# adaLN decode block with cached GQA attention: w_mod loaded over two DMA queues by halves of the partitions, and the last two parts of wo loaded as one transfer

## The chip, the cores and the metric

The kernel runs on one core of one Trainium2 chip. The metric is the device time of one execution in microseconds. The engines are named as in the profile: PE (TensorE), DVE (VectorE), ACT (ScalarE), POOL (GpSimd) and SP (SyncE). SP does no arithmetic here; it issues DMAs.

## What is computed

One token goes through a transformer block in decode. A modulation vector comes from a condition `c`; attention has 32 query heads over 8 KV heads with a cache of 32768 positions; a ReLU feed-forward part follows. All inputs are bf16. The k and v caches are 64 MB each and make up nearly all of the bytes.

```python
x = A_x                                              # [1, 1, 512]
mod = (silu(c) @ w_mod).reshape(1, 6, 1, 512)        # w_mod [512, 3072]
sa, ca, ga, sb, cb, gb = (mod[:, i] for i in range(6))
h = layernorm(x) * (1 + ca) + sa
q = (h @ wq) -> 32 heads of 128                      # wq [512, 4096]
scores = q @ k.T * 128 ** -0.5                       # k, v [8, 32768, 128], 4 query heads share one
o = softmax(scores) @ v
x = x + ga * (o @ wo)                                # wo [4096, 512]
h = layernorm(x) * (1 + cb) + sb
x = x + gb * (relu(h @ w1) @ w2)                     # w1 [512, 1792], w2 [1792, 512]
```

## The kernel before

**The stream.** All large tensors come in one fixed order, the list `stream` (L139 to L144): `w_mod`, `wq`, the two halves of head 0's K, then for each head in turn half of the next head's K and half of this head's V, at the end the last V in three pieces, `wo` in four parts (`WOP`, L47: heads 0 to 3, 4 and 5, 6, 7), `w1` in two and `w2` in six. `need(key)` (L147) issues loads in this order until the wanted one has been issued. Each load is one DMA from SP (`stream_dma`, L131, the DMA at L132) into one of five slots of 32 KB per partition (`ring`, L74). A slot's next load waits on SP until the last user of the slot is done. A K or V half is 4096 KB: 128 partitions of 32 KB each, contiguous in memory. `w_mod` is 3072 KB: partition p holds rows 4p to 4p + 3, 24,576 contiguous bytes. A wo part of one head is 512 KB: 4096 bytes for each partition. Completion of SP's and ACT's DMAs is counted on eight semaphores taken in turn, so a DMA may also wait for the one eight places before it.

**The head.** While `w_mod` comes, POOL loads `c` and `x` as small rows (L156, L157), DVE builds masks, and PE turns c and x into columns (L227). ACT and DVE make `siluT` (L284 to L289), PE multiplies it with `w_mod` (`to_rows`, L295), and rows become columns again (L313). The first layer norm gives `hT` (L278), PE multiplies it with `wq` (L362), and `qrep_sb` (L377) holds q. ACT writes q into a block-diagonal operand `qbd` for each head (`build_qbd`, L389).

**The heads.** For each K half DVE transposes four pieces in place (`turn_k`, L405), PE forms scores (`scores`, L422), DVE takes them out with their maximum (L428), and a softmax with one exponential (L459) and one transpose (L465) gives `PT_g`. P·V is 32 matmuls for each half of V (`pv`, L484), in a loop on PE's sequencer for all but the last pieces. The order on PE and DVE is written out by hand in L599 to L742: scores of head g + 1 run between the parts of head g.

**The tail.** After the last V, `project(i)` multiplies the heads of part i with their part of `wo`. Parts 0 and 1 use it as the moving operand (L561), parts 2 and 3 as the weights that are loaded into PE (L567). `keep_clock(n)` puts n filler matmuls (L597) between these steps. Then come the second norm, `w1` (L714), the ReLU (L725), `w2` (L735) and the output DMA (L743).

Of the kernel before, what the change touches and what calls it, by code (L numbers as in the profile page):

```python
# [17 lines left out]
def kernel(  # L18
# [14 lines left out]
    nc = tc.nc  # L33
    P = 128
    _, _, D = A_x.shape
    _, Hkv, Sk, Dh = A_k_cache.shape
    Hq = A_wq.shape[1] // Dh
    REP = Hq // Hkv
# [8 lines left out]
    WOP = [(0, Hkv // 2), (Hkv // 2, Hkv // 4), (Hkv - 2, 1), (Hkv - 1, 1)]  # L47
    WOROWS = 2
    LAST = Hkv - 1
# [11 lines left out]
    vv = A_v_cache[0].rearrange("g (p j) d -> g p j d", p=P)  # L61
    wm_v = w_mod.rearrange("(p kt) n -> p kt n", p=P)
    wq_v = A_wq.rearrange("(p kt) n -> p kt n", p=P)
    def wo_v(i):
        g0, n = WOP[i]
        return A_wo[g0 * REP * Dh:(g0 + n) * REP * Dh, :].rearrange("(p r) d -> p r d", p=P)

    w1_v = B_w1.rearrange("(p kt) f -> p kt f", p=P)
    w2_v = B_w2.rearrange("(p f) d -> p f d", p=P)

# [15 lines left out]
    loaded, last_loop = {}, []  # L86
# [3 lines left out]
    def piece(name, at, n):  # L90

        if name not in pieces:
            pieces[name] = ring.tile([P, 2 * TK * Dh], BF16, tag="slot", name=name)
        return pieces[name][:, at:at + n]

    def load(key):
        kind = key[0]
        if kind == "wm":
            t = ring.tile([P, KT, 6 * D], BF16, tag="slot", name="wm_sb")
            src = wm_v  # L100
        elif kind == "wq":
            t = ring.tile([P, KT, Hq * Dh], BF16, tag="slot", name="wq_sb")
            src = wq_v
        elif kind in "kv":
            g, steps = key[1], key[2]
            src = (kv if kind == "k" else vv)[g, :, TK * steps[0]:TK * (steps[-1] + 1), :]
            name = "Ksb" if kind == "k" else "Vsb"
            if len(steps) == 2:
                t = ring.tile([P, TK * len(steps), Dh], BF16, tag="slot", name=name)
            else:  # L110
                t = piece(name, TK * Dh * (steps[0] % 2), TK * Dh).rearrange("p (j d) -> p j d", d=Dh)
        elif kind == "wo":
            g0, n = WOP[key[1]]
            t = piece("wo_sb", g0 * REP * D, n * REP * D).rearrange("p (r d) -> p r d", d=D)
            src = wo_v(key[1])
        elif kind == "w1":
            k0, k1 = W1P[key[1]]
            t = piece("w12_sb", k0 * Dff, (k1 - k0) * Dff).rearrange("p (kt f) -> p kt f", f=Dff)
            src = w1_v[:, k0:k1]
        else:  # L120
            f0, f1 = W2P[key[1]]
            t = piece("w12_sb", KT * Dff + f0 * D, (f1 - f0) * D).rearrange("p (f d) -> p f d", d=D)
            src = w2_v[:, f0:f1]
        stream_dma(t[:], src)
        if kind in "kv":
            for i, u in enumerate(steps):
                loaded[(kind, g, u)] = t[:, TK * i:TK * (i + 1), :]
        else:
            loaded[key] = t[:]

    def stream_dma(dst, src):  # L131
        i = nc.sync.dma_start(out=dst, in_=src)  # L132
        tc.stamp_issue_order_token(i.ins, "sp_stream")
        if last_loop:

            tc.add_manual_dep(i.ins, last_loop[0], mybir.DependencyInfo(
                mybir.DependencyClass.NoSync, mybir.DependencyReason.DATA))

    stream = [("wm",), ("wq",)] + [("k", 0, (2 * G, 2 * G + 1)) for G in range(NG)]  # L139
    for g in range(LAST):  # L140
        for G in range(NG):
            stream += [(kind, gg, (2 * G, 2 * G + 1)) for kind, gg in (("k", g + 1), ("v", g))]
    stream += [("v", LAST, (0, 1)), ("v", LAST, (2,)), ("v", LAST, (3,))] + [("wo", i) for i in range(len(WOP))]
    stream += [("w1", i) for i in range(len(W1P))] + [("w2", i) for i in range(len(W2P))]  # L144
    pos = [0]

    def need(key):  # L147
        while key not in loaded:
            load(stream[pos[0]])
            pos[0] += 1  # L150
        return loaded[key]
# [17 lines left out]
    for hp in range(4):  # L169
        h, par = hp // 2, hp % 2  # L170
        src = AP(ib.tensor, ib.offset + 64 * h + par, [[ib.ap[0][0], P], [0, 4], [2, 32]])
# [8 lines left out]
        out=mask4, in_=ident_f[:].rearrange("p (x q) -> p q x", q=REP), op=ALU.add, axis=AX.X,  # L180
# [3 lines left out]
    for n in sorted({n * REP for _, n in WOP}):  # L184
        cmask[n] = const.tile([P, P // n], F32, name=f"cmask{n}")
        nc.vector.tensor_reduce(
            out=cmask[n][:], in_=ident_f[:].rearrange("p (c r) -> p c r", r=n), op=ALU.add, axis=AX.X,
# [3 lines left out]
            out=rsel_f[:], in_=ident_f[:].rearrange("p (c r) -> p r c", r=n), op=ALU.add, axis=AX.X,  # L191
# [6 lines left out]
        out=smask[:], in_=ident_f[0:16, 0:16].rearrange("p (s q) -> p s q", q=REP), op=ALU.add, axis=AX.X,  # L198
# [8 lines left out]
        out=place32[:], in_=ident_f[:].rearrange("p (j m) -> p m j", m=32), op=ALU.add, axis=AX.X,  # L207
# [3 lines left out]
        out=rowpick[:], in_=ident_f[:].rearrange("p (j m) -> p j m", m=32), op=ALU.add, axis=AX.X,  # L211
# [10 lines left out]
        out=cx_bd[:], in0=cx_row[:].unsqueeze(1).to_broadcast([16, 8, D // 8]),  # L222
# [108 lines left out]
    def four_rows(e, name):  # L331
# [15 lines left out]
        out=nca[:], in0=modT_sb[:, KT:2 * KT], scalar1=-1.0, scalar2=-1.0, op0=ALU.mult, op1=ALU.add,  # L347
# [3 lines left out]
        out=ncb[:], in0=modT_sb[:, 4 * KT:5 * KT], scalar1=-1.0, scalar2=-1.0, op0=ALU.mult, op1=ALU.add,  # L351
# [16 lines left out]
    for i in range(2):  # L368
        nc.vector.transpose(out=q_cols[:, i, :], in_=q_ps[i])
        nc.scalar.copy(  # L370
            out=qT_sb[:, 16 * i:16 * (i + 1)], in_=q_cols[:, i, :].rearrange("p (h r) -> p h r", r=32)[:, :, 0],
# [227 lines left out]
    with tc.manual_schedule(engines={mybir.EngineType.PE, mybir.EngineType.DVE}):  # L599
# [11 lines left out]
        for g in range(LAST):  # L611
# [81 lines left out]
            out=x1T[:], in0=x1T[:], scalar=1.0, in1=xT, op0=ALU.mult, op1=ALU.add, accum_out=stat2[:, 0:1],  # L693
# [29 lines left out]
        for f0, f1 in ((0, FT // 2), (FT // 2, FT)):  # L723
            nc.vector.transpose(out=hidT[:, f0:f1], in_=hid_v[:, f0:f1])  # L724
            nc.scalar.activation(  # L725
                out=AP(hb.tensor, hb.offset + KT * KT * f0, [hb.ap[0], [KT * KT, f1 - f0], [KT + 1, KT]]),
                in_=hidT[:, f0:f1, 0:1].to_broadcast([P, f1 - f0, KT]), func=ACT.Relu,
# [46 lines left out]
```

## Time and profile before

| | |
|---|---|
| Runs | 355.38, 355.42, 355.53 us; median 355.42 |
| The profiled execution | 355.74 us, its span 353.9 us |
| Busy | PE 279.8 us (79%), DVE 203.1 (57%), ACT 25.4 (7%), POOL 3.9 (1%) |
| DMA | 149.59 MB, mean 423 GB/s |
| Granted PE clock | 0.947 mean |
| w_mod | one issue from SP, 3072 KB, 10.4 us to landing |
| wq | 4096 KB, 19.6 us to landing |
| wo | 2048, 1024 and twice 512 KB; 29.1, 31.1 and 32.3 us (median of the two) to landing |

The span runs from the first to the last instruction; the time of an execution holds a little more around it. A line of the timeline gives start, duration, engine, line of the kernel, operation, output and inputs, count, and in brackets the idle time before and what ended it. A line of the windows gives the stretch, its length, busy time and number of instructions for PE, PEld (weight loads), DVE, ACT and POOL, then the granted clock, the DMA share and GB/s.

### The profile page before, as it was taken

Reading aid. Unit: us, or ns where it says so; the run is one execution under the profiler, and the core shown is the slowest. Engines: PE = TensorE matmul, PEld = TensorE weight load, DVE = VectorE, ACT = ScalarE, POOL = GpSimd, SP = SyncE. Lnnn points to the kernel's source line nnn. Section 1 sums busy time; section 2 is a strip of 40 time slices with the busy share of each in tenths; the row PEclk is TensorE's granted clock in tenths of the full one; section 3 lists DMA queues with packets and bytes.
Section 4 is the critical chain, followed back from the end, with each engine's and each line's share of the span. In section 5 each row is a group of like instructions: output and inputs, shape, how many; then the busy total and the mean of one; then the engine's idle time right before and its main releaser. Section 6 shows DMA issues by size and latency. Waiting matters only on the chain. (4 is left out here: it accounts for less than half of the span.)

```text
span 353.9 us, 4006 instructions
## 1 busy us (share of the span) xinstructions
PE 279.8 (79%) x1311; PEld 112.7 (32%) x1311; DVE 203.1 (57%) x271; ACT 25.4 (7%) x69; POOL 3.9 (1%) x16
## 2 busy tenths in 40 slices
PE   0542781999898979897979796979689687989996
PEld 0221230333343323332323232323234233334444
DVE  6245775882768268462939178553938095734142
ACT  1220003000010001000100001000100010002000
POOL 4000000000000000000000000000000000000000
PEclk9995997799899999998999899999999997999999
DMA  8999999999999999999999999999999999999994
GB/s 309 455 422 445 431 422 441 441 418 424 459 418 422 459 418 424 441 437 426 433 444 417 430 456 419 427 446 426 422 448 430 422 439 441 422 430 424 421 420 177
DMA packets 6852, 149.59 MB, mean 423 GB/s; under 512 B 824, under 2 KB 1080, under 8 KB 1976
## 3 DMA queue, kind: packets, MB, share of 16 engines
q1 hardware_dynamic: 6776, 149.43, 98.4%
q8 instruction: 8, 0.13, 0.1%
q14 instruction: 4, 0.03, 0.0%
q0 software_dynamic: 64, 0.00, 0.0%
HBM read 149.42 MB, written 0.00 MB: 422 GB/s over the span
## 5 line engine op out<-in xcount | busy, mean ns | idle before, releaser
L405 DVE STREAM_TRANSPOSE Ksb<-Ksb 128x2048 f32<-128x2048 f32 x64 | 142.9, 2281 | 63.9 <-DMA Ksb<-in_A_k_cache_dram 63.9
L484 PE MATMUL o_ps<-Vsb,PT_g 128*16 (+1 forms) x512 | 130.0, 395 | 21.5 <-ACT qbd L389 7.2
L422 PE MATMUL S_ps<-Ksb,qbd 128*128 128x512 bf16 x512 | 121.8, 388 | 23.5 <-DVE Ksb L405 21.9
L422 PEld LDWEIGHTS <-qbd 128*128 128x128 bf16 x512 | 49.0, 98 | 87.6 <-issue 31.8
L484 PEld LDWEIGHTS o_ps<-Vsb,PT_g 128*16 x416 | 37.4, 90 | 90.2 <-issue 63.7
L428 DVE TENSOR_SCALAR_CACHE_REDUCE S_g<-S_ps 128x512 f32<-128x512 f32 x16 | 11.0, 690 | 34.4 <-PE S_ps L422 34.4
L389 ACT COPY qbd<-qrep_sb 32x16 bf16<-32x16 bf16 x32 | 6.4, 201 | 138.7 <-PE S_ps L422 137.6
L465 DVE STREAM_TRANSPOSE PT_g<-P_g 128x1024 bf16<-128x1024 bf16 x8 | 9.7, 1218 | 6.6 <-ACT P_g L459 6.6
L484 PEld LDWEIGHTS <-PT_g 128*16 128x16 bf16 x96 | 8.2, 90 | 11.0
L456 ACT ACTIVATE nbias<-Mb_ps 128x1 f32<-128x1 f32 x8 | 1.4, 171 | 136.8 <-PE Mb_ps L454 136.8
L459 ACT ACTIVATE P_g<-S_g,nbias 128x1024 bf16<-128x1024 f32 x8 | 9.2, 1148 | 0.2
L227 PE MATMUL xc_ps<-cx_sel,cx_bd 16*128 16x2 bf16 x4 | 0.3, 172 | 11.1 <-DVE cx_bd L221 11.1
L515 DVE SCALAR_TENSOR_TENSOR Y<-o_ps,smask,Y 16x128 f32<-16x128 f32 x24 | 8.1, 339 | 0.8
L471 PE MATMUL L_ps<-Lexp,ones_f 128*128 128x4 f32 x16 | 3.0, 257 | 4.3 <-DVE Lexp L468 4.3
L597 PE MATMUL spare_ps<-qbd,ident_bf 128*128 128x512 bf16 x19 | 5.6, 380 | 0.0
L440 PE MATMUL mT_ps<-ident_f,m_p 128*1 128x128 f32 x8 | 2.2, 270 | 3.9 <-DVE m_p L437 2.0
L471 PEld LDWEIGHTS L_ps<-Lexp,ones_f 128*128 128x128 f32 x16 | 3.1, 221 | 5.8 <-issue 5.1
L443 DVE TENSOR_REDUCE Mrow<-mT_ps 1x4 f32<-1x128 f32 x8 | 2.1, 257 | 4.6 <-PE mT_ps L440 4.6
L534 DVE TENSOR_TENSOR oT_sb<-acc_ps,Linv 128x4 bf16<-128x4 f32 x8 | 1.2, 150 | 5.7 <-PE acc_ps L521 5.7
L295 PE MATMUL mod_ps<-wm_sb,siluT 128*1 128x512 bf16 x24 | 3.6, 624 | 1.0 <-DVE siluT L289 1.0
L505 DVE MEMSET o_ps<- 16x512 f32 x8 | 3.9, 485 | 0.8
L552 DVE CAST o_sb<-o_ps 128x4 bf16<-128x4 f32 (+2 forms) x4 | 0.7, 167 | 5.7 <-PE o_ps L548 5.7
(115 smaller groups left out, 80.0 us busy)
## 6 DMA issues: line engine op xcount, KB each, us to landing
Ksb<-in_A_k_cache_dram SPq DMA_DIRECT2D x16, 4096.0 KB, 35.6
Vsb<-in_A_v_cache_dram SPq DMA_DIRECT2D x15, 4096.0 KB, 35.2
wq_sb<-in_A_wq_dram SPq DMA_DIRECT2D x1, 4096.0 KB, 19.6
Vsb<-in_A_v_cache_dram SPq DMA_DIRECT2D x2, 2048.0 KB, 31.8
wm_sb<-in_w_mod_dram SPq DMA_DIRECT2D x1, 3072.0 KB, 10.4
wo_sb<-in_A_wo_dram SPq DMA_DIRECT2D x1, 2048.0 KB, 29.1
w_sb<-in_B_w_dram SPq DMA_DIRECT2D x1, 1344.0 KB
wo_sb<-in_A_wo_dram SPq DMA_DIRECT2D x1, 1024.0 KB, 31.1
```

Of the source, the lines that this page charges most:

```text
L295: nc.tensor.matmul(dst[j // 4][32 * (j % 4):32 * (j % 4) + 1, :], lhsT=src_T[:, kt:kt + 1], rhs=w[:, kt, j * 512:(j + 1) * 512], start=(kt ...
L389: nc.scalar.copy(out=o, in_=i)
L405: t = nc.vector.transpose(out=KTt.bitcast(F32), in_=KTt.bitcast(F32))
L422: nc.tensor.matmul(S_ps_tiles[g], lhsT=qbd[g % 2][:, hp, 4 * (7 - s):4 * (7 - s) + P], rhs=KTv[:, 16 * sl:16 * sl + 16, h, :, par], start= ...
L428: nc.vector.tensor_scalar(out=S_tiles[g][:, G, :], in0=S_ps_tiles[g], scalar1=1.0, scalar2=None, op0=ALU.mult, op1=ALU.max, accum_out=m_ti ...
L459: nc.scalar.activation(out=P_g[:], in_=S_g[:].rearrange("p g f -> p (g f)"), func=ACT.Exp, bias=nbias[:], scale=scale, accum_out=l_g[:],)
L465: nc.vector.transpose(out=PT_g[:], in_=P_g[:])
L471: nc.tensor.matmul(L_ps[:], lhsT=ones_f[:], rhs=Lexp[:], start=True, stop=True)
L484: nc.tensor.matmul(o_tiles[g][:], lhsT=PT, rhs=Vx, start=False, stop=False, skip_group_check=True)
L505: nc.vector.memset(o_tiles[g][:], 0.0)
L515: nc.vector.scalar_tensor_tensor(out=Y[:], in0=o[:, s], scalar=smask[:, s:s + 1], in1=Y[:], op0=ALU.mult, op1=ALU.add,)
L597: nc.tensor.matmul(spare[0], lhsT=ident_bf[:], rhs=qbd[0][:, :, 0:P], start=True, stop=True)
```

## The change

`w_mod` is loaded by two DMAs: SP takes partitions 0 to 63, and ACT, as its first instruction, partitions 64 to 127. Each partition's bytes are the same. The parts 2 and 3 of `wo` (heads 6 and 7, 512 KB each) come as one transfer of 1024 KB, 128 partitions with two runs of 4096 bytes each. The total number of DMAs from SP and ACT stays the same. The instructions of PE, DVE and POOL and their order are unchanged; ACT has the one DMA more. Lines below the edit are four higher in the changed kernel.

```diff
-    def wo_v(i):
-        g0, n = WOP[i]
-        return A_wo[g0 * REP * Dh:(g0 + n) * REP * Dh, :].rearrange("(p r) d -> p r d", p=P)
-
...
         elif kind == "wo":
-            g0, n = WOP[key[1]]
-            t = piece("wo_sb", g0 * REP * D, n * REP * D).rearrange("p (r d) -> p r d", d=D)
-            src = wo_v(key[1])
+            parts = key[1]
+            (g0, n), m = WOP[parts[0]], len(parts)
+            t = piece("wo_sb", g0 * REP * D, m * n * REP * D).rearrange("p (g x) -> p g x", g=m)
+            src = A_wo[g0 * REP * Dh:(g0 + m * n) * REP * Dh, :].rearrange("(g p r) d -> p g (r d)", g=m, p=P)
...
-        stream_dma(t[:], src)
+        if kind == "wm":
+            stream_dma(t[0:P // 2], src[0:P // 2])
+            nc.scalar.dma_start(out=t[P // 2:P], in_=src[P // 2:P])
+        else:
+            stream_dma(t[:], src)
...
+        elif kind == "wo":
+            for m, i in enumerate(parts):
+                loaded[("wo", i)] = t[:, m].rearrange("p (r d) -> p r d", d=D)
...
-    stream += [("v", LAST, (0, 1)), ("v", LAST, (2,)), ("v", LAST, (3,))] + [("wo", i) for i in range(len(WOP))]
+    stream += [("v", LAST, (0, 1)), ("v", LAST, (2,)), ("v", LAST, (3,))] + [("wo", parts) for parts in ((0,), (1,), (2, 3))]
```

## Prediction

> **What bounds the kernel now.** I began with the page's queue summary and its line of DMA shares, then cut the first microseconds and the long middle into windows, and last read the timeline and the waits around the two places that the change touches.
>
> ```profile
> q1 hardware_dynamic: 6776, 149.43, 98.4%
> ...
> 30.00:100.00 70.00, 51.63 (x201) 20.03 (x202) 48.09 (x38) 4.30 (x12) 0.00 (x0) 0.86 1.01 433
> 100.00:200.00 100.00, 86.88 (x371) 34.33 (x369) 62.30 (x70) 6.66 (x21) 0.00 (x0) 0.98 1.00 433
> 200.00:300.00 100.00, 82.49 (x340) 32.17 (x340) 59.49 (x70) 5.04 (x13) 0.00 (x0) 0.96 1.00 432
> ```
>
> One queue, SP's, carries all the bulk data and keeps its 16 DMA engines busy for 98.4% of the span. In the windows the last two columns are the DMA share and GB/s: 433 GB/s from 30 to 300 us, 27.1 GB/s for each engine, with no hole. A 4096 KB transfer lands 35 us after its issue, so three or four are always queued. Whatever delays this stream delays all behind it, one for one.
>
> The timeline shows how the stream becomes the end:
>
> ```profile
> 283.51 6.70 DVE L405 STREAM_TRANSPOSE Ksb<-Ksb 128x2048 f32<-128x2048 f32 x3 [7.53 <-DMA Ksb<-in_A_k_cache_dram]
> ...
> 298.65 4.63 PE L484 MATMUL o_ps<-Vsb,PT_g 128*16 x12 [0.66 <-PE L_ps L471]
> ...
> 302.99 2.31 DVE L405 STREAM_TRANSPOSE Ksb<-Ksb 128x2048 f32<-128x2048 f32 x1 [4.50 <-DMA Ksb<-in_A_k_cache_dram]
> ```
>
> DVE stands idle 7.53 us for head 7's first half of K, and at 283.51 starts on it. From there one chain of DVE and PE work runs to the output DMA at 351.84 us: transposes, the softmax of head 6, its P·V loop from 298.65, scores, the last P·V, the projections and the feed-forward part. So the end is the landing of that K plus some 68 us. The last K half (302.99) is covered: its scores begin only at 307.78.
>
> **The head: w_mod over two queues.** Before, one 3072 KB transfer, issued at 0.74 us and landed 10.4 us later. Now SP issues 64 partitions and ACT the other 64. The number of bytes does not change, and neither does SP's issue count here (one DMA, 0.40 us).
>
> ACT gets one DMA issue in front of its table load. Queued behind it are that load (0.74 to 2.02 us before) and the exponential of L284, which starts at 11.58 after 9.56 us of idle; an issue of 0.4 us costs nothing there. Without that cover it would cost its 0.4 us.
>
> The half transfers also make two landings where SP's first V load and PE's w_mod matmuls waited for one. The V load went out at 17.13 us with w_q and three K halves queued, good until about 40 us; a delay of 10 us is covered. The PE matmuls wait today for siluT at 13.52, 2.4 us after w_mod at 11.1.
>
> The two small rows c and x (GpSimd's queue, landing at 8.4 and 10.2 us) have to share the engines with one more queue. The third queue is there only until w_mod has landed, so their 8.3 us can grow by a few, not double; siluT, hT and q would move with them. In the timeline q is spread into qbd by 26.80, while PE's first scores wait for K, landed and transposed, until 32.79: 6 us of cover, which grows with every delay of the stream. I cost it at nothing; beyond the 6 us each would cost one at the first scores.
>
> That leaves what two half-width transfers do to the stream itself. These windows of a quarter microsecond show its start (a packet is counted where it starts):
>
> ```profile
> 1.75:2.00 0.25, 0.00 (x0) 0.00 (x0) 0.23 (x1) 0.25 (x1) 0.25 (x2) 1.00 5.36 1278
> 2.00:2.25 0.25, 0.00 (x0) 0.00 (x0) 0.00 (x0) 0.02 (x1) 0.25 (x1) 1.00 1.53 295
> ...
> 4.00:4.25 0.25, 0.00 (x0) 0.00 (x0) 0.25 (x2) 0.00 (x0) 0.25 (x2) 1.00 0.23 98
> 4.25:4.50 0.25, 0.00 (x0) 0.00 (x0) 0.25 (x2) 0.00 (x0) 0.25 (x1) 1.00 2.28 983
> 4.50:4.75 0.25, 0.00 (x0) 0.00 (x0) 0.25 (x2) 0.00 (x0) 0.25 (x3) 1.00 1.14 492
> 4.75:5.00 0.25, 0.00 (x0) 0.00 (x0) 0.25 (x2) 0.00 (x0) 0.24 (x2) 1.00 0.00 0
> ```
>
> Read as bytes, the first two rows are 393 KB, and so are the three from 4.00: 16 rows of w_mod (24,576 bytes each), one for each engine. The engines march in step: a wave starts within half a microsecond, then nothing starts until the next. At 27.1 GB/s a row lasts 0.91 us, and w_mod is eight rows for each engine, 7.27 us.
>
> Before, each wave went to partitions of both halves. Now, if all 16 engines take a row from SP's queue, the wave goes to partitions 0 to 63 only, and the next, from ACT's, to 64 to 127 only. No row of the trace shows a large transfer over 64 partitions, so I bound it. From below: if only the engines limit, nothing is lost, and something could be won at the cold start (a rival below). From above: no transfer here ever gave a partition more than its 1/128 of 433 GB/s. If that is a limit of the receiving side, a wave over half of the partitions takes twice as long, 8 x 0.91 = 7.3 us in all. Engines that share a destination collide less the further they are apart: half a microsecond, the width of a wave, would leave 0.41 of 0.91 us of loss in each row, 3.3 us in all. I take the middle of 3.3 and 7.3, 5.3 us, because waves this narrow put both queues' rows in step, and because a transfer has landed only when its slowest engine is done.
>
> The Trainium skill, page "SBUF — State Buffer", section "Door 1: The DMA port swizzle", states that partitions 0 to 63 reach only 8 of 16 SBUF ports (196 GB/s measured for them), and that two concurrent transfers, at partition 0 and partition 64, gave just 6% more than one. By that, an estimate, 3.15 MB at 208 GB/s would take 15.1 us and the head lose 7.9 us; this trace has nothing that could confirm it.
>
> **The tail: wo's two last parts in one transfer.** One issue fewer for SP. The bytes stay, and their place in the queue. SP's later issues move up (they wait for one of eight completion slots, and these now count one transfer further back), but the last of them still waits for this very transfer, and the queue is full anyway: nothing.
>
> What changes is when the second last part is known to have landed. Before, the four wo loads were issued from 307.8 to 309.1 and took 29.1 to 32.7 us, so the last landed at 309.1 + 32.7 = 341.8. The part before it is 512 KB shorter in line, 1.2 us at 433 GB/s: 340.6. Its user:
>
> ```profile
> 341.20 0.59 PE L597 MATMUL spare_ps<-qbd,ident_bf 128*128 128x512 bf16 x2
> ...
> 341.42 0.80 PEld L567 LDWEIGHTS <-wo_sb 128*128 128x128 bf16 x16
> ```
>
> These weight loads begin at 341.42, inside the filler matmuls that end at 341.80. Merged, they cannot begin before 341.8: between 0.1 us (the filler covers most) and 0.45 us (0.38 and a weight load) are added. Queued behind them on PE are project(2), the joining of rows, project(3), the norm and the feed-forward matmuls; nothing absorbs it, and the output waits for all. I take 0.3 us, nearer to the upper end, as the loads had run ahead of the filler by 0.38. The stream and this chain move together, so this holds whatever the head does.
>
> **Sum.** The profiled execution took 355.74 us, 1.8 more than its span and 0.32 above the median. 355.74 + 5.3 + 0.3 = 361.3; against the median 355.42 + 5.6 = **361.0 us**. Own range of this case: 355.42 + 3.3 + 0.1 to 355.42 + 7.3 + 0.45, 358.8 to 363.2.
>
> **Rivals.** *The halves cost the stream nothing* (0.25). For it: an engine's 27.1 GB/s is the same for every size of row, which fits a limit in the engines; then eight rows per engine are eight rows, from whichever queue. The Trainium skill, page "DMA: Bandwidth & Descriptors", section "Issuing engines are not separate DMA queues", says that the same 16 engines serve all issuers and that only issue time is saved; the 98.4% on one queue and the 0.40 us issue agree with that. The time is 355.42 + 0.3 = 355.7 (355.2 to 356.3). Against it: narrow waves, as above.
>
> *The cold start shrinks* (0.12), the other side. The first wave starts at 1.75, and the third only at 4.25, where two rows at 0.91 would have put it at 3.6; and w_mod lands at 11.1, where 1.75 + 7.27 is 9.0. Up to 2.1 us of start are lost on the slowest engine. If a second queue's row is fetched while the first is still cold, part of that comes back. With 1.2 us won and 0.3 lost the time is 354.5; it is faster by over 0.2% from 1.0 us won on. At its end, 2.1, it is 353.6. Against it: the following row of the same queue could be fetched ahead as well, and the gap is there all the same.
>
> *The engines fall out of step early* (0.08): after one or two rows some take SP's half while others take ACT's, and only 0.9 to 2.3 us are lost: 356.6 to 358.0.
>
> One thing widens every case by up to 1 us: the granted clock was 0.50 from 296 to 300 us, on the chain to the end (eight scores took 2.77 us there, 1.90 elsewhere); a moved start can move that dip.
>
> **How the numbers follow.** Collision 0.55, nothing 0.25, cold start 0.12, out of step 0.08. The forecast is the likeliest, 361.0. The range, 355.0 to 363.2, holds the collision, the second case and the one out of step, and leaves out the cold start and edges, under 2 in 10. About 0.2%, 0.7 us, is what a measurement of this kernel can tell from no change. Faster by more: 0.12. Within it: 0.22, nearly all of the second case. Slower: 0.66, the collision, out of step, and 0.03 of the second.
>
> **What would show it.** Right: w_mod's landing near 16 us instead of 11.1, windows from 2 to 16 us well under 400 GB/s, the first transpose of K near 36 instead of 30.48, and the wait for head 7's K ending near 289 instead of 283.51; the span from there to the output up by 0.3, with the wo_sb weight loads after the landing. Wrong: w_mod landed by 11 us at 400 GB/s and over, which leaves only the tail; or K's first transpose before 30 us, which is the cold start. The tail is wrong if the output still comes 68.3 us after that K wait.

## The result: 363.29 us, 2.2% slower

The changed kernel takes 363.29 us (median of six runs, 361.87 to 364.51) against 355.40 for the kernel before (355.23 to 355.53); the ratio is 1.0225 with a 95% interval of 1.0213 to 1.0238. That is 7.9 us. The direction and the place were forecast, the size was not: 361.0 with an upper end of 363.2. The profiled execution took 363.29 us with a span of 361.5, so the two profiled executions differ by 7.55 us.

**The profile after.** The queue summary of the changed kernel has a second row, ACT's queue:

```profile
q1 hardware_dynamic: 6696, 147.85, 96.3%
q10 hardware_dynamic: 80, 1.57, 2.0%
```

One window over the head of the kernel before, and then the windows of the changed kernel (last columns: granted clock, DMA share, GB/s):

```profile
4.75:9.75 5.00, 0.00 (x0) 0.00 (x0) 3.27 (x19) 0.00 (x0) 0.24 (x2) 1.00 0.94 400
```

```profile
4.75:9.75 5.00, 0.00 (x0) 0.00 (x0) 3.27 (x19) 0.00 (x0) 0.24 (x2) 1.00 0.97 211
...
12.00:14.00 2.00, 0.00 (x0) 0.00 (x0) 0.00 (x0) 0.00 (x0) 0.00 (x0) 1.00 0.97 197
14.00:16.00 2.00, 0.00 (x0) 0.00 (x0) 0.00 (x0) 0.00 (x0) 0.00 (x0) 1.00 0.97 197
...
2.75:16.00 13.25, 0.00 (x0) 0.00 (x0) 4.89 (x19) 0.00 (x0) 2.23 (x9) 1.00 1.02 217
```

Here the two columns part company. The DMA share is 0.97, so by that column all engines are busy; but they move 197 to 211 GB/s in these windows and 217 on average, where the kernel before moved 400 in the window 4.75 to 9.75. A busy DMA engine is not one at its rate; GB/s has to be read beside the share. In windows of a quarter microsecond a row of w_mod is seen to take twice its time:

```profile
5.50:5.75 0.25, 0.00 (x0) 0.00 (x0) 0.25 (x2) 0.00 (x0) 0.00 (x0) 1.00 4.34 885
...
6.25:6.50 0.25, 0.00 (x0) 0.00 (x0) 0.25 (x3) 0.00 (x0) 0.00 (x0) 1.00 1.85 393
...
7.25:7.50 0.25, 0.00 (x0) 0.00 (x0) 0.25 (x3) 0.00 (x0) 0.00 (x0) 1.00 2.65 590
7.50:7.75 0.25, 0.00 (x0) 0.00 (x0) 0.25 (x3) 0.00 (x0) 0.00 (x0) 1.00 1.76 393
```

A packet is counted, with its bytes and its time, in the window in which it starts. At 5.50 the 885 GB/s are nine rows of 24,576 bytes, and the share of 4.34 is 4.34 x 0.25 us x 16 engines, 17.4 us in all: 1.93 us a row. The six rows at 7.25 come to 1.77 us each; before, a row took 0.91. So it is not that half of the engines stand idle: all 16 work, and each row takes twice as long.

The timelines show where this goes. The kernel before:

```profile
30.48 2.31 DVE L405 STREAM_TRANSPOSE Ksb<-Ksb 128x2048 f32<-128x2048 f32 x1 [5.51 <-DMA Ksb<-in_A_k_cache_dram]
...
351.84 0.35 SPq L743 DMA_DIRECT2D out_dram<-o_bf  x1
```

The changed kernel:

```profile
38.36 4.50 DVE L409 STREAM_TRANSPOSE Ksb<-Ksb 128x2048 f32<-128x2048 f32 x2 [4.69 <-DMA Ksb<-in_A_k_cache_dram]
...
290.94 6.70 DVE L409 STREAM_TRANSPOSE Ksb<-Ksb 128x2048 f32<-128x2048 f32 x3 [6.42 <-DMA Ksb<-in_A_k_cache_dram]
...
349.18 0.61 PEld L571 LDWEIGHTS <-wo_sb 128*128 128x128 bf16 x16 [1.60 <-DMA wo_sb<-in_A_wo_dram]
...
359.42 0.35 SPq L747 DMA_DIRECT2D out_dram<-o_bf  x1
```

w_mod's slower half lands at 18.7 us (SP's half, 18.0 us after its issue) instead of 11.1. The first K is transposed from 38.36 instead of 30.48, 7.88 us later, and head 7's first K from 290.94 instead of 283.51, 7.43 us later: of the delay only 0.45 us was made up in between. From there to the output DMA it is 68.48 us, before it was 68.33: 0.15 more. 7.43 + 0.15 = 7.58 us, which is the 7.55 us between the two profiled executions but for 0.03.

### The profile page after: what moved, and what is told of

Its sections match the earlier page's. It is cut to its first block, busy times and chain, and to the rows that moved or that the text cites. A ratio compares the mean times of both kernels' runs of the same rounds, so it can differ in the third digit from the quotient of the medians.

```text
span 361.5 us, 4008 instructions
## 1 busy us (share of the span) xinstructions
PE 281.5 (78%) x1311; PEld 112.0 (31%) x1311; DVE 202.9 (56%) x271; ACT 25.4 (7%) x69; POOL 3.9 (1%) x16
## 5 line engine op out<-in xcount | busy, mean ns | idle before, releaser
L488 PE MATMUL o_ps<-Vsb,PT_g 128*16 (+1 forms) x512 | 127.8, 382 | 21.9 <-ACT qbd L393 9.0
L426 PE MATMUL S_ps<-Ksb,qbd 128*128 128x512 bf16 x512 | 125.1, 397 | 20.2 <-DVE Ksb L409 18.7
L426 PEld LDWEIGHTS <-qbd 128*128 128x128 bf16 x512 | 49.9, 100 | 86.5 <-issue 32.7
L488 PEld LDWEIGHTS o_ps<-Vsb,PT_g 128*16 x416 | 36.0, 86 | 90.0 <-issue 65.8
```

What stands on the lines that cost most here:

```text
L426: nc.tensor.matmul(S_ps_tiles[g], lhsT=qbd[g % 2][:, hp, 4 * (7 - s):4 * (7 - s) + P], rhs=KTv[:, 16 * sl:16 * sl + 16, h, :, par], start= ...
L488: nc.tensor.matmul(o_tiles[g][:], lhsT=PT, rhs=Vx, start=False, stop=False, skip_group_check=True)
```

## The experiments

The theory was: a transfer into partitions 0 to 63, or 64 to 127, is received at half of the rate, so w_mod takes its time once more and the whole stream stands later by that. Rivals: the second queue itself costs something; the reading side; a one-time cost of the start; the merged wo transfer.

**w_mod alone split, wo in four parts.** The edit is made to the kernel before.

```diff
+        if kind == "wm":
+            stream_dma(t[0:P // 2], src[0:P // 2])
+            nc.scalar.dma_start(out=t[P // 2:P], in_=src[P // 2:P])
+        else:
+            stream_dma(t[:], src)
-        stream_dma(t[:], src)
```

> The kernel before with w_mod alone split by halves of the partitions over SP and ACT; wo stays in four parts. If the head carries the whole loss (half-width transfers run at half rate), head 7's first K is waited for until about 290.9 us as in the changed kernel, 7.4 us later than before, and the time is 362.4 to 363.0 us, 0.3 to 1.1 us below the changed kernel's 363.3, since PE's wait of 1.1 us for the merged wo transfer is gone. If the tail carried much of the loss, the time would be below 360 us.

Measured: 363.53 us (363.30 to 363.81), ratio 1.0227 (1.0211 to 1.0243). Its timeline:

```profile
291.03 6.70 DVE L409 STREAM_TRANSPOSE Ksb<-Ksb 128x2048 f32<-128x2048 f32 x3 [7.64 <-DMA Ksb<-in_A_k_cache_dram]
...
359.37 0.35 SPq L747 DMA_DIRECT2D out_dram<-o_bf  x1
```

The head carries the loss: 7.52 us at that K, and from there 68.34 us to the output, as before. (The rest of this run's 8.1 us lies behind the issue of the output, where the span goes on for 2.4 us instead of 2.1, and in the 0.3 us by which the profiled execution before lay above its median.) The expected gain over the changed kernel did not show: 363.53 against 363.29, within the spread of the latter's own runs. So in the changed kernel PE's wait of 1.11 us for wo (1.60 for its weight loads) was not on top: from K to the end of the filler, PE had come through 1.15 us faster (290.94 to 348.08, before 283.51 to 341.80), and waited that away.

**wo alone merged.** The edit takes the split of w_mod out of the changed kernel.

```diff
         if kind == "wm":
-            stream_dma(t[0:P // 2], src[0:P // 2])
-            nc.scalar.dma_start(out=t[P // 2:P], in_=src[P // 2:P])
+            stream_dma(t[:], src)
```

> The kernel before with wo's two last parts as one transfer and w_mod whole. The prediction's tail term stands alone: weight loads of wo that began at 341.42 us wait for the landing at 341.8, plus 0.1 to 0.45 us, 355.7 us. Rival: the filler matmuls cover it all, 355.4 us. Second rival: the merged transfer itself lands later than the last part did, plus 1 us, as PE's wait of 1.1 us in the changed kernel would have it.

Measured: 355.86 us against 355.45, ratio 1.0013 (1.0004 to 1.0022): plus 0.1 to 0.8 us, 0.4 at the middle. The timeline of this kernel has the wait that was forecast:

```profile
341.63 0.61 PEld L570 LDWEIGHTS <-wo_sb 128*128 128x128 bf16 x16 [0.48 <-DMA wo_sb<-in_A_wo_dram]
```

The weight loads, which nothing held back before, now wait 0.48 us for the landing. The output leaves at 351.87, 68.51 us after the K (which was waited for until 283.36), 0.18 more than before. The mechanism is as predicted; the size lies within the range of the term, but for the upper end of the interval.

**Two queues, but all partitions in each.** From here on the edits are made to the kernel before again.

```diff
+        if kind == "wm":
+            stream_dma(t[:, 0:KT // 2], src[:, 0:KT // 2])
+            nc.scalar.dma_start(out=t[:, KT // 2:KT], in_=src[:, KT // 2:KT])
+        else:
+            stream_dma(t[:], src)
-        stream_dma(t[:], src)
```

> The kernel before with w_mod over SP and ACT, but split by its rows within a partition: each of the two transfers covers all 128 partitions with 12,288 bytes each. If the loss comes from the half of the partitions, it is gone: w_mod lands by about 11 us, 433 GB/s from the start, 355.4 us give or take 0.5. If it comes from two queues that feed the same engines at once, it stays: 362 to 363 us. If a second queue shortens the cold start, 354.5 us.

Measured: 355.62 us against 355.45, ratio 1.0009 (1.0000 to 1.0018). The windows of this kernel:

```profile
4.75:9.75 5.00, 0.00 (x0) 0.00 (x0) 3.27 (x19) 0.00 (x0) 0.24 (x2) 1.00 1.01 428
```

428 GB/s from two queues at once; SP's half of w_mod landed 10.4 us after its issue, as the whole did before, and the first K was transposed from 30.84 us, no earlier than before (30.48). So the second queue costs nothing that shows at head 7's K (283.36, before 283.51), and it does not shorten the cold start either: that rival falls here.

**One queue, but half of the partitions in each transfer.**

```diff
+        if kind == "wm":
+            for p0 in (0, P // 2):
+                stream_dma(t[p0:p0 + P // 2], src[p0:p0 + P // 2])
+        else:
+            stream_dma(t[:], src)
-        stream_dma(t[:], src)
```

> The kernel before with both halves of w_mod's partitions issued by SP, one after the other, so there is one queue and the two halves are never in flight together by design. If a half-width transfer runs at half rate by itself, the loss stays: about 7.3 us, 362.5 to 363 us, windows of about 210 GB/s from 3 to 17 us. If the loss needs two queues whose rows collide, it is gone: 355.4 us.

Measured: 363.46 us, ratio 1.0223 (1.0208 to 1.0239), the same loss without ACT's queue. Its windows:

```profile
4.75:9.75 5.00, 0.00 (x0) 0.00 (x0) 3.28 (x19) 0.00 (x0) 0.25 (x2) 1.00 0.92 192
```

From 2.75 to 16 us it is 217 GB/s, exactly what the two queues of the changed kernel moved, and head 7's K is waited for until the same 290.94. The second queue gained nothing over one.

**Which 64 partitions.** First the middle ones:

```diff
+        if kind == "wm":
+            for p0, p1 in ((32, 96), (0, 32), (96, 128)):
+                stream_dma(t[p0:p1], src[p0:p1])
+        else:
+            stream_dma(t[:], src)
-        stream_dma(t[:], src)
```

> The kernel before with w_mod in three transfers, all from SP: partitions 32 to 95 first, then 0 to 31, then 96 to 127. If what counts is which partitions are written (0 to 63 and 64 to 127 have separate ways in, and 32 to 95 uses both), the first transfer runs at full rate, 3.6 us for 1.57 MB, and the other two at half, 7.3 us together: plus 3.6 us, 359.1 us. If only the number of partitions counts (64 at half, 32 at half or a quarter of the rate), plus 7.3 to 14.5 us, 362.7 to 370 us.

Measured: 360.97 us against 355.37, ratio 1.0161 (1.0139 to 1.0182). The windows of this kernel, the first with partitions 32 to 95 in flight, the second with 0 to 31 and 96 to 127:

```profile
4.00:6.00 2.00, 0.00 (x0) 0.00 (x0) 2.00 (x7) 0.00 (x0) 0.99 (x4) 1.00 0.98 418
...
8.00:12.00 4.00, 0.00 (x0) 0.00 (x0) 0.02 (x1) 0.00 (x0) 0.00 (x0) 1.00 1.12 240
```

64 partitions in the middle run at 418 GB/s, 32 at one end at a time at 240 (211 in the window from 8 to 13 us). So the number does not decide, the place does. The time of 5.6 us over before is 2 us more than worked out from this and less than the other theory's 7.3; the rates in the windows decide between them. At head 7's K the delay is 5.26 us, 1.7 more than the 3.6 worked out, so the 2 us arise in the stream for the most part; they are not accounted for.

Then the even and the odd ones, over two queues:

```diff
+        if kind == "wm":
+            stream_dma(t[0:P:2], src[0:P:2])
+            nc.scalar.dma_start(out=t[1:P:2], in_=src[1:P:2])
+        else:
+            stream_dma(t[:], src)
-        stream_dma(t[:], src)
```

> The kernel before with w_mod over SP and ACT, SP taking the even partitions and ACT the odd ones: 64 partitions each, but spread over the whole 128. If what counts is that both halves are reached by a transfer, nothing is lost: 355.4 to 355.8 us. If 64 partitions are slow however they lie, or the DMA engines' shares still meet in pairs, the loss of the changed kernel stays: 362.5 to 363.5 us.

Measured: 355.90 us against 355.37, ratio 1.0016 (1.0006 to 1.0026). The windows of this kernel:

```profile
4.75:9.75 5.00, 0.00 (x0) 0.00 (x0) 3.27 (x19) 0.00 (x0) 0.24 (x2) 1.00 1.02 433
```

Two transfers of 64 partitions on two queues, as in the change, and full rate: the loss is gone, but for half a microsecond. That rest has no counterpart in the profiled execution (355.73 us, before 355.74) or at its K wait (283.48, before 283.51), and its cause stays open.

**More of the same: wq split as well.** The edit is that of w_mod alone, with both tensors in the condition:

```diff
-        if kind == "wm":
+        if kind in ("wm", "wq"):
```

> The split of the changed kernel for w_mod and for wq as well (partitions 0 to 63 from SP, 64 to 127 from ACT); wo in four parts. If half-width transfers run at half rate, each byte moved so costs its full-rate time once more: 4.19 MB at 433 GB/s, 9.7 us on top of the 363.5 us with w_mod alone, 373.2 us. If the loss is a one-time cost of the start or of the second queue, it stays at 363.5 us.

Measured: 372.91 us, ratio 1.0484 (1.0462 to 1.0507): 9.4 us over the 363.53 with w_mod alone, 9.7 had been worked out. The window of this kernel from 12 to 30 us, where the one before moved 436 GB/s, shows the half rate go on through wq:

```profile
12.00:30.00 18.00, 4.93 (x33) 2.13 (x34) 2.74 (x12) 2.37 (x4) 0.00 (x0) 1.00 1.01 219
```

**The reading side.** All partitions, half of the memory range in each transfer. Its rows meet other elements of `silu(c)` than they should, so this kernel gives the time of the loads and not the block's result:

```diff
+        if kind == "wm":
+            for h in range(2):
+                stream_dma(t[:, 2 * h:2 * h + 2], w_mod.rearrange("(h p kt) n -> h p kt n", h=2, p=P)[h])
+        else:
+            stream_dma(t[:], src)
-        stream_dma(t[:], src)
```

> The kernel before with w_mod in two transfers from SP, each into all 128 partitions, but each from one contiguous half of w_mod's rows in memory (row 256h + 2p + k goes to partition p; so the rows meet other elements of silu(c) than they should). If the loss comes from the side that is written, there is none: 355.4 to 355.8 us. If it comes from reading only one half of the memory range at a time, it is there: about 362.7 us.

Measured: 355.63 us against 355.37, ratio 1.0009 (0.9999 to 1.0018). Its window:

```profile
4.75:9.75 5.00, 0.41 (x5) 0.36 (x5) 4.31 (x24) 0.20 (x1) 0.24 (x2) 1.00 1.06 449
```

Reading one half of w_mod's range at a time costs nothing that can be measured; the loss lies with the side that is written.

## Why the prediction was right about the mechanism and wrong about the size

**What bounds the kernel** held. Of the delay of 7.88 us at the first K, 7.43 was still there at head 7's K at 291 us, and the 68 us behind it stayed within 0.2 us. The prediction's own check, the K wait, told nearly the whole result.

**The head: the step that failed is the middle between 3.3 and 7.3 us.** The collision of the halves is shown: it comes with the halves of the partitions (one queue too), goes when each transfer reaches both halves (by columns, by even and odd), and grows with the bytes (w_mod 8.1 us in time, wq another 9.4). The term was 5.3 us; at the K wait it measured 7.43, the upper end. The mistake was to credit the engines for being out of step, with up to 0.41 us in each row. The waves did stand apart, even in two groups 0.8 us from each other (885 GB/s at 5.50, 393 at 6.25, 590 and 393 around 7.5), and the rows in these windows took 1.76 to 1.93 us all the same.

The packets that the trace counts for each queue show what the prediction had not foreseen. From 1 to 6.9 us 48 rows of w_mod start, and all are ACT's; from 6.9 to 8.6 us 16, all SP's; from 8.6 to 10.4 us 16, all ACT's; and the last 48 are SP's. With eight rows for each of 16 engines, that comes to three rows an engine for partitions 64 to 127, one for 0 to 63, one for 64 to 127 and three for 0 to 63. An engine that is half a microsecond late mostly meets others that write to the same half, just as with SP's queue alone, where the cost is the same. Only at the three changes of queue are some engines in one half and some in the other, and there little was gained: 1.77 us a row at 7.25, where it was 1.93 at 5.50. How far out-of-step engines would gain if the halves alternated row by row, as the prediction had it, no run here shows.

The upper end itself was taken at exactly half of 433, 217 GB/s; from 2.75 to 16 us it was 217 on average and 197 in the worst windows. With 7.4 for 5.3 the prediction's sum would have been 355.42 + 7.4 + 0.3 = 363.1, the measured time less 0.2 us.

The Trainium skill, page "SBUF — State Buffer", section "Door 1: The DMA port swizzle", had been weighed and put aside as unconfirmed; the half rate measured here agrees with it. The 6% for two transfers over one stand in the Trainium skill's section "Can I just issue two DMAs to hit both halves?" of the same page; the 208 GB/s worked out from them, an estimate, lie near the 217 measured here. The head's 7.9 us by that estimate are nearer to the measured 7.43 than my 5.3. In this case two queues moved 217 GB/s, and one queue moved the same 217. By the mapping of partitions to ports in the Trainium skill's section "Door 1: The DMA port swizzle", 32 to 95 reach all 16, with which the 418 GB/s above agree. The sentence "The only way to hit all 16 ports is one transfer spanning all 128 partitions" in the Trainium skill's section "Can I just issue two DMAs to hit both halves?" does not hold here: partitions 32 to 95 alone ran at 418 GB/s, and the even and the odd ones, as two transfers, at 433.

**What was costed at nothing in the head** stayed at nothing, with one size wrong. ACT's issue took 0.55 us with 16.69 us of idle behind it. SP's V load went out at 24.84, well before the queue could run dry. (The prediction had the queue good until about 40 us; wq and three K halves of 9.7 us each behind w_mod's landing at 11.1 are good until about 50, which only adds cover.) But the small rows c and x did nearly double, x from 8.3 to 16.0 us to landing, where I had said they could not; siluT, and not w_mod, was then again the last input of the w_mod matmuls (21.2 us). The cover was there, because the stream was late as well: qbd was done at 35.5 and the first scores began at 40.7.

**The tail** was right: 0.3 us expected, 0.4 (0.1 to 0.8) measured alone, by the wait that was named. In the changed kernel it is 0.15 us in the trace, and that is a balance of two things. The prediction had allowed up to 1 us for a moved clock dip, and the dip did move. The windows from 296 us, the kernel before and then the changed one (third column from the end: granted clock):

```profile
296.00:300.00 4.00, 3.34 (x11) 1.54 (x10) 1.12 (x6) 0.00 (x0) 0.00 (x0) 0.50 0.93 401
```

```profile
296.00:300.00 4.00, 4.00 (x20) 1.68 (x18) 3.75 (x9) 1.13 (x2) 0.00 (x0) 1.00 0.97 414
```

In the changed kernel it was 1.00 in every window from 283 to 315 us, PE came through 1.15 us faster to the end of the filler, and then waited for wo. What each is worth can be read from the other runs. Three of them had no dip from 283 to 315 us either, with wo in four parts (by columns, even and odd, half of the memory range): they took 68.00 to 68.01 us from the K to the output, 0.33 less than the kernel before. Against these the changed kernel's 68.48 puts the merged transfer at 0.48 us. So the tail's 0.15 is 0.48 less 0.33; that the dip moved away was luck.

**The rivals.** The second, halves that cost nothing, falls with w_mod alone split. The cold start falls with the columns, where a second queue had all its chance and the first K came no earlier. The one out of step falls with the rows of 1.76 to 1.93 us and with the order of the queues above. The signs and the chances pointed the right way; the range was cut at the upper bounds of its two terms, without the 1 us that the prediction itself gave for the clock dip and without anything for the spread of the runs, 361.87 to 364.51, and that left the result out by 0.1 us. Why the changed kernel's runs spread so far, and those with w_mod alone split only from 363.3 to 363.8, stays open.

None of the kernels tried is faster than the one before. The experiments point to leaving both loads as they were.

## What to carry to other kernels

Divide a load between queues by columns or by every second partition, never by the halves 0 to 63 and 64 to 127: each such half ran at about 217 GB/s here instead of 430, whichever queue it came from, and on a stream that is never idle nearly all of the loss arrives at the end. Dividing it gained nothing here in any form. When two bounds are far apart, ask in which order the queues will serve the engines' rows, before taking the middle. And merging transfers makes the user of the first piece wait for the last one, here 0.4 us.

## What the runs showed of the hardware that was not expected

The DMA share stayed at 0.97 while the rate was halved, so a full queue in that column says nothing of the rate. Where the 64 partitions lie decides: 0 to 63 and 64 to 127 gave 192 to 211 GB/s from 4.75 to 9.75 us, 32 to 95 gave 418, and every second one 433. Of two transfers that were issued together on two queues, 48 rows of ACT's started first, then 16 of SP's, 16 of ACT's and 48 of SP's; they did not take turns row by row. Two rows of 1 KB in GpSimd's queue took 13.0 and 16.0 us to land instead of 7.1 and 8.3 while the slow halves were in flight, and with SP's queue alone 10.0 and 12.8.
